# Two more blocks of the first mixer product, and one more down pair in each of the last two blocks, computed with seven products in place of eight, in an order given as a list

## The chip, the cores and the metric

The kernel runs on one core of a Trainium2 chip. The metric is the device time of one execution in microseconds (us), the median of three runs. Beside the runs there is one profiled execution. Its engines are TensorE (PE, with its weight loads PEld), VectorE (DVE), ScalarE (ACT), GpSimd (POOL) and SyncE (SP, which issues most DMAs).

## The reference

The input x has 2048 tokens of 512 channels. Linear attention over 32 heads of 16 channels is multiplied by a gate; the gate comes from a mixer that shifts channel groups along the tokens, and from an MLP with 1376 hidden channels behind it.

```python
xn = _layernorm(x)
s = _A_ref(xn, A_wqkv, A_wo)                       # linear attention, phi(t) = t+1 or exp(t), + 1e-6
g = _silu(_B_ref(xn, B_w1, B_w2, B_w3, B_w4))
return x + s * g

def _B_ref(x, w1, w2, w3, w4):
    h = _gelu(_layernorm(x) @ w1)                  # first mixer product
    ...                                            # its four groups of 128 channels, shifted +1, -1, +2, -2 tokens
    x1 = x + hs                                    # hs = shifted h @ w2
    return x1 + _gelu(_layernorm(x1) @ w3) @ w4    # up, down
```

## The kernel before

The 2048 tokens are cut into four **blocks** of 512 (`BT`), each of four tiles of 128. Every fp32 value that goes into a product is split into a rounded high half and a low half (`rounded`: ACT copies the high half, DVE subtracts it for the low one), and each product of two values is three matmuls: high by high, low by high, high by low (`products`). A matmul streams 512 or 256 columns.

Where a product can be cut into two by two quarters, `seven` (and its kin) forms seven products of sums of quarters in place of eight of the quarters themselves: the left sums are `s1` to `s4`, the right ones `t1` to `t4`, and three PSUM banks `pa`, `pb`, `pe` collect them in halves of 256 columns. Before the change this is done for keys and queries of blocks 1 to 3 (`keys_queries`, banks `pak`, `pbk`, `pek`), for the second mixer product (`mix2`, banks `pam`, `pbm`, `pem`), for the attention output, for the up products, and for as many **down pairs** of a block as `SEVENS = 0, 2, 3, 3` says (`stream` and `chain`, banks `a` and `uc`); the other down pairs go plainly (`plain`, 512 columns).

The first mixer product is plain in every block. `mix1(b, g)` makes one group of 128 channels: twelve matmuls of 512 columns into the bank `h`, over the four channel chunks, with the tokens read one or two places to the side, which is the shift; four columns beside each block hold the neighbours' tokens (`split_halo`). DVE multiplies the bank by the row `abc` of each token's scale (`ht<-h,abc`; `join_a` fetches that row, spread over the partitions, from the row `arow` in DRAM), and ACT takes the Gelu. `make_u(b)` before that subtracts the token means (`um`, fetched from `mrow`) from the turned tokens `xt`, splits them, and forms the sums `us`, which keys and queries of that block use. Layernorm's statistics come from DVE's batch-norm instructions (`moments`). The weights w1 are split once, their halves stored to DRAM (`W1D`) and fetched again for blocks 2 and 3 (`w1_for`).

The whole program is recorded as a list of operations (`Plan`), and `Plan.emit` puts them in order: it plans times from modelled durations, gives each operation a due time, nudges some by the table `SOONER`, and chooses buffers as they come free. `ORD` sets the order in which the parts of the first half are recorded. TensorE runs attention's first products and the mixer of block 0 first, then blocks 1 to 3, then the MLP of the blocks one after the other.

Of the kernel before, what the change touches and what calls it, by code (L numbers as in the profile page):

```python
# [15 lines left out]
P = 128  # L16
# [72 lines left out]
class Plan:  # L89
# [121 lines left out]
    def move(self, eng, out, src, kind, mb, reads, writes, emit):  # L211
        op = self.add(eng, .42 if eng == "SP" else .6, 0, reads, writes, emit, mb=mb)
        op.rate, op.tail = self.RATE[kind], self.TAIL.get(kind, 0.0)
        return op
# [13 lines left out]
    def gather(self, out, src, share=1.0, kind="gather"):  # L228
# [3 lines left out]
    RATE = {"load": 2.93, "fetch": 3.3, "half": 4.27, "row": 4.23, "turn": 5.4, "store": 2.45,  # L232
            "gather": 5.73, "quarter": 6.42}

    def landing(self, op, s, dma):

        soft = op.eng == "POOL"
        dma = max(dma, s + (.33 if soft else 0)) + op.mb * op.rate
        late = min(1.11, .68 * max(0.0, dma - s))
        return dma, max(dma + (1.36 if soft else 1.25) + late, s + (3.77 if soft else 1.97 if op.loads else 1.68)) + op.tail  # L240

    GAP = {"PE": .16, "ACT": .035, "DVE": .035, "POOL": .15, "SP": .035}
    BEGIN = {"PE": 1.0, "ACT": 2.0, "DVE": .8, "POOL": .8, "SP": .75}
    DMA0 = 2.2
    TABLE, EXTRA = 1.41, .22
    TAIL = {"row": .95}
    PATIENCE = 2.5
    COLD, COLD_TILL = 1.84, 5.8
    SAFE = 2.0
# [3 lines left out]
    def nudged(self, table):  # L253

        for n, k in zip(table[::2], table[1::2]):
            self.ops[n].due -= .25 * k
        self.backward()

    def deadlines(self, first):
        t = first  # L260
        for op in self.ops:
            if op.eng == "PE":
                op.nom = t
                t += op.busy
        for op in self.ops:
            op.due = op.nom if op.eng == "PE" else INF
        self.backward()
        for op in self.ops:
            op.at = max([p.at + p.lat for p in op.pre], default=0.0)
            if op.eng == "PE":  # L270
                op.at = op.nom
            elif any(t.psum for t in op.tiles):
                op.due = min(op.due, op.at + self.PATIENCE)
            elif op.soon:
                op.due = min(op.due, max(op.at, op.soon.at) + op.patience)
            elif op.due == INF and not op.post:
                op.due = op.at + op.patience
        self.backward()

    def backward(self):  # L280
        for op in reversed(self.ops):
            if op.eng != "PE":
                for o in op.post:
                    op.due = min(op.due, o.due - self.GAP[o.eng] - (6.0 + op.mb * 4 if op.mb else op.lat))

    def meets(self, op, slots, users):

        e = {o.eng for o in op.pre}
        n = Counter()
        for t in op.tiles:  # L290
            if t.ap is None and t.tag in slots and n[t.tag] < len(slots[t.tag]):
                e |= users.get((t.tag, slots[t.tag][n[t.tag]][1]), set())
                n[t.tag] += 1
        return len(e - {"ACT"}) > 1

    def emit(self, first, lead, reserve, window, ahead, table=()):
        self.deadlines(first)
        self.nudged(table)
        ops = self.ops
        waiting = {op: len(op.pre) for op in ops}  # L300
        avail = {e: [] for e in ("PE", "ACT", "DVE", "POOL", "SP")}
        for op in ops:
            op.ready = 0.0
            if not waiting[op]:
                avail[op.eng].append(op)
        pe = [op for op in ops if op.eng == "PE"]
        head = 0
        free = dict(self.BEGIN)
        slots = {tag: [(0.0, i) for i in range(n)] for tag, n in self.counts.items()}
        port, dma = 0.0, self.DMA0  # L310
        lock = [(-1.0, -1.0)] * 8
        under = [0.0] * 8, [0.0] * 8
        table = 0
        users = {}
        done = set()
        slip = 0.0
        left = len(ops)
        while left:
            while head < len(pe) and pe[head] in done:
                head += 1  # L320
            front = pe[head] if head < len(pe) else None
            slip = max(0.0, free["PE"] - front.nom) if front else INF
            best = None
            for e, cands in avail.items():
                picks = []
                low = INF
                for op in cands:
                    s = max(free[e], op.ready)
                    if op.mb:
                        s = max(s, under[e == "POOL"][0] + self.GAP[e])  # L330
                    s = max(s, op.floor)
                    if op.two and s < port:
                        s = port
                    if e == "POOL" and not op.mb and not op.two:
# [23 lines left out]
                    if not ok:  # L358
                        continue
# [1443 lines left out]
```

## Time and profile before

| | us |
|---|---|
| median of 3 runs (501.72, 501.77, 502.53) | 501.77 |
| the profiled execution's span | 501.2 |
| TensorE busy in it | 494.3 (99%) |
| VectorE busy | 440.9 (88%) |
| ScalarE busy | 388.9 (78%) |
| DMA moved | 116.69 MB |

The span is the time from the first to the last instruction of one profiled execution, of which we have one; the runs' times hold 0.57 us more at the median. Busy is the time in which an engine had an instruction of its own in work. A busy engine is the bound only where the others don't hold it up, so the share has to be read by stretch.

### The profile page before, as it was taken

The page shows a single profiled execution, that of the slowest core. Times are in us where ns is not written, and L with a number is a line of the kernel's source. Part 1 is how long each engine was busy: PE and PEld are TensorE (multiplying, and loading weights), DVE is VectorE, ACT ScalarE, POOL GpSimd, SP SyncE. Part 2 cuts the span into 40 slices and gives each one's busy share as a digit, 9 for nine tenths or more (in the row PEclk, how much of TensorE's full clock was granted, in tenths as well). Part 3 has the DMA queues.
Part 4 walks back from the last instruction along what each step waited for, and adds up shares of the span by engine and source line. Part 5 has one row for each costly group of instructions (what it writes and reads, how often), then busy time and mean ns, then how long its engine had stood idle before and what let it go on. Part 6 is the DMA issues. An engine that isn't in the chain of part 4 may idle for free.

```text
span 501.2 us, 9464 instructions
## 1 busy us (share of the span) xinstructions
PE 494.3 (99%) x3102; PEld 442.2 (88%) x3102; DVE 440.9 (88%) x944; ACT 388.9 (78%) x859; POOL 84.9 (17%) x97
## 2 busy tenths in 40 slices
PE   8999999999999999999999999999999999999996
PEld 6777887898888888899999989999899998999986
DVE  5989999999699995999999998897799969998364
ACT  5999899867798884977777579957699878977551
POOL 1344433131221122020100002200020200201100
PEclk9999999999999999999999999999999999999999
DMA  7949985479994799979897599978699887898604
GB/s 245 365 110 239 319 261 144 106 149 269 322 260 134 191 336 233 262 198 286 266 319 243 193 312 260 269 235 245 190 252 305 225 192 239 278 314 266 154 8 120
DMA packets 86989, 116.69 MB, mean 233 GB/s; under 512 B 8864, under 2 KB 41148, under 8 KB 86940
## 3 DMA queue, kind: packets, MB, share of 16 engines
q1 hardware_dynamic: 77004, 98.00, 60.3%
q0 software_dynamic: 9936, 18.09, 20.9%
q8 instruction: 24, 0.39, 0.3%
q14 instruction: 25, 0.20, 0.2%
HBM read 73.70 MB, written 32.91 MB: 213 GB/s over the span
## 4 chain that ended last, share of the span: by engine, by line
PE 88%; DMA 8%; SPq 1%; ACT 1%; issue 0%; DVE 0%; POOL 0%; DVEq 0%
PE a L151 15%; PE pb L151 11%; PE h L151 9%; PE pbk L151 7%; PE g L151 7%; PE acc L151 6%; PE pe L151 6%; DMA w1t<-in_w 5%; PE pbm L151 5%; PE pbs L151 4%; PE uc L151 3%; PE pek L151 3%; PE pa L151 3%; PE pem L151 2%; PE pes L151 2%; PE pak L151 2%
## 5 line engine op out<-in xcount | busy, mean ns | idle before, releaser
L230 POOL DMA_DIRECT2D th<-in_x x14 | 12.3, 926 | 164.4 <-DMA w_t<-w4t 75.6
L230 POOL DMA_DIRECT2D o<-x x16 | 14.1, 895 | 65.1 <-DVE o L198 48.0
L178 ACT ACT_TABLE_LOAD x18 | 23.1, 1283 | 0.3
L652 POOL TENSOR_TENSOR rs<-w,nhalf 128x4 f32<-128x4 f32 (+2 forms) x10 | 16.7, 1675 | 38.1 <-DVE w L203 38.1
L173 ACT ACTIVATE gf<-gf 128x256 f32<-128x256 f32 (+1 forms) x48 | 22.0, 469 | 1.2 <-DVE gf L198 0.8
L230 POOL DMA_DIRECT2D zacc<-kr x16 | 16.4, 1022 | 36.5 <-DMA zacc<-kr 13.2
L230 POOL DMA_DIRECT2D e<-x1d x12 | 10.6, 1084 | 62.0 <-DVE e L198 44.1
L208 DVE SCALAR_TENSOR_TENSOR kr<-kt,kr 128x512 f32<-128x512 f32 x16 | 11.0, 686 | 4.4 <-ACT kt L173 4.4
L173 ACT ACT_TABLE_LOAD x11 | 14.1, 1283 | 1.0 <-PEq L1794 0.8
L173 ACT ACTIVATE ht<-ht 128x512 f32<-128x512 f32 x16 | 9.8, 623 | 6.5 <-DVE ht L198 6.5
L646 DVE BATCH_NORM_STATS2 st<-o 128x6 f32<-128x512 f32 x16 | 10.6, 681 | 4.7 <-DMA o<-x 4.7
L198 DVE TENSOR_TENSOR e<-a,e 128x512 f32<-128x512 f32 (+1 forms) x17 | 9.7, 587 | 5.1 <-PE a L151 5.1
L198 DVE TENSOR_TENSOR th<-th,so 128x512 f32<-128x512 f32 (+1 forms) x17 | 10.9, 648 | 3.3 <-ACT th L173 3.3
L173 ACT ACTIVATE x<-x,nm,rs 128x512 f32<-128x512 f32 x16 | 12.9, 805 | 0.0
L173 ACT ACTIVATE p<-pe 128x256 f32<-128x256 f32 x20 | 7.6, 382 | 6.7 <-PE pe L151 6.5
L173 ACT ACTIVATE p<-pb 128x256 f32<-128x256 f32 x20 | 7.6, 381 | 6.7 <-PE pb L151 6.5
L173 ACT ACTIVATE y<-o,nm,rs 128x512 f32<-128x512 f32 x16 | 11.8, 804 | 1.2 <-DVE nm L208 1.2
L173 ACT ACTIVATE th<-e 128x512 f32<-128x512 f32 (+1 forms) x12 | 7.1, 608 | 7.1 <-DVE e L198 7.1
L208 DVE SCALAR_TENSOR_TENSOR pq<-pq,qr 128x512 f32<-128x512 f32 x12 | 8.2, 686 | 3.9 <-ACT pq L173 3.8
L198 DVE TENSOR_TENSOR ht<-h,abc 128x512 f32<-128x512 f32 x16 | 10.8, 681 | 0.4 <-PE h L151 0.4
L198 DVE TENSOR_TENSOR gf<-pb,p 128x256 f32<-128x256 f32 x20 | 8.4, 418 | 3.1 <-PE pb L151 3.0
L208 DVE SCALAR_TENSOR_TENSOR qz<-pq,zb 128x512 f32<-128x512 f32 x16 | 10.7, 684 | 0.2
(1868 smaller groups left out, 2285.1 us busy)
## 6 DMA issues: line engine op xcount, KB each, us to landing
w_s<-in_w SPq DMA_DIRECT2D x34, 256.0 KB, 4.8
w_t<-w4t SPq DMA_DIRECT2D x26, 256.0 KB, 4.5
w_b<-w4d SPq DMA_DIRECT2D x24, 256.0 KB, 5.3
x<-in_x SPq DMA_DIRECT2D x16, 256.0 KB, 6.3
zacc<-kr POOLq DMA_DIRECT2D x16, 256.0 KB, 4.8
o<-x POOLq DMA_DIRECT2D x16, 256.0 KB, 4.7
x1d<-o SPq DMA_DIRECT2D x16, 256.0 KB, 3.8
xt<-in_xt SPq DMA_DIRECT2D x15, 256.0 KB, 6.2
```

The costliest lines, as they stand in the source:

```text
L151: lambda: nc.tensor.matmul(out.get(), lhs.get(), rhs.get(), start=start, stop=stop, skip_group_check=more))
L173: nc.scalar.activation(out.get(), src.get(), func, scale=get(scale), **kw)
L178: op.warm = lambda: nc.scalar.activation(self.scr[1].get(), self.scr[0].get(), func)
L198: self.vec(eng, out, [a, b], lambda: self.e(eng).tensor_tensor(out.get(), a.get(), b.get(), op=op), True)
L208: lambda: self.nc.vector.scalar_tensor_tensor(out.get(), a.get(), get(s), b.get(), op0=op0, op1=op1),
L230: lambda: self.nc.gpsimd.dma_start(out.get(), get(src), accum_op=ALU.add))
L646: pl.add("DVE", .62, .69, [xv], [st], lambda: nc.vector.bn_stats(st.get(), xv.get()))
L652: lambda: g.tensor_tensor(out.get(), src.get(), nh.get(), op=ALU.pow))
```

## The change

In blocks 2 and 3, `mix1_pair(b, p)` makes two groups of 128 channels at once by `seven`: the token quarters and sums that keys and queries already use stand on the left, and seven forms of w1 on the right (`b11`, `t1`, `b21`, `t2`, `b22`, `t3`, `t4`, for each of two pairs `p`). `forms_w1` makes the four sums on DVE and stores them to `W1D`; `mix1_pair` fetches all seven forms of 512 columns for each pair and block, 14 fetches a block for 8 before. In block 1, `mix1_whole` stays plain; block 0 keeps `mix1` with the multiplication by `abc`.

So that the scale no longer has to follow the product, `make_u` multiplies the centred tokens by `abc`, and keys and queries of these blocks use another factor (`rk` for `rs1`). The tokens are read unshifted; the shift is made later by an offset into `ht`, whose ends are copied between neighbouring blocks (`edges`), and so `forms(b)` waits for the mixer of block b+1, and `ORD` puts the second mixer products later. The statistics of blocks 2 and 3 go from DVE to ACT (`totals`: two passes with a running sum each). `SEVENS` becomes 0, 2, 4, 4, and the last block holds back two groups of down products, not three (`keep`). `Plan.emit` no longer plans: it follows `ORDER`, a list of all operations, and `HOMES`, a list of buffers.

```diff
-    SEVENS = 0, 2, 3, 3
+    SEVENS = 0, 2, 4, 4
...
+    def totals(xv, t, mv):
+        m = mv.cols(0, 1)
+        pl.act(t, xv, AF.Copy, scale=1.0 / D, total=m)
+        k = -float(D) if t is xv else -1.0
+        pl.act(t, xv, AF.Square, scale=k, bias=m, total=mv.cols(1, 2))
...
+        a = piece(f"abc{b}")
+        o = EDGE + b * BT
+        pl.fetch(a, arow[:, o:o + BT].via(lambda ap: ap.to_broadcast([P, BT])), "row")
         for c in range(NC):
-            pl.tt(XT[b, c], XT[b, c], m, ALU.subtract)
+            pl.tt(XT[b, c], XT[b, c], m, ALU.add)
+            pl.tt(XT[b, c], XT[b, c], a, ALU.mult)
...
+    def edges(b, n):
+        t, d = HT[b, n], -SHIFT[ORDER[n]]
...
+    def mix1_whole(b, g):
+        ps = bank(f"h{b}_{g}")
+        products(ps, [HELD[0].chunk(c, g * P, (g + 1) * P) + ut(b, c, 2, 2 + BT) for c in range(NC)])
+        t = HT[b, ORDER.index(g)] = pl.new("p", f"ht{b}_{g}", F32, PIECE)
+        pl.act(t[:, 2:2 + BT], ps, AF.Gelu_apprx_tanh)
+
+    def mix1_pair(b, p):
...
+        w = {y: pl.new("p", f"w1{y}_{p}{b}", F32R, PIECE)[:, :512] for y in W1F}
+        for k, y in enumerate(W1F):
+            o = (p * len(W1F) + k) * 512
+            pl.fetch(w[y].f32, W1D[:, o:o + 512])
+        def prod(x, y):
+            return [(w[y].cols(c * P, (c + 1) * P), w[y].cols((2 + c) * P, (3 + c) * P)) + U[b][x][c] for c in range(2)]
+        ps = seven(f"g{b}_{p}", z, prod)
+        pl.act(z[0], z[0], AF.Gelu_apprx_tanh)
+        pl.act(hs[1], hs[1], AF.Gelu_apprx_tanh)
+        pl.act(hs[0].cols(TH, BT), ps, AF.Gelu_apprx_tanh)
...
+        for k in range(4):
+            hl = rounds(f"w1t{k}")
+            rounded(*hl, t[k])
+            for q in range(2):
+                keep_w1(f"t{k + 1}", q, None, hl[q])
...
-            moments(f"st{i}", v, mv1[:, 2 * i:2 * i + 2])
+            totals(v, v, mv1[:, 2 * i:2 * i + 2])
...
-        keep = 3 if last else 2
+        keep = 2
...
-    pl.emit(first=6.0, lead={"p": 14.0, "w": 14.0}, reserve={"p": 20, "w": 1}, window=12.0,
-            ahead=6.0, table=SOONER)
...
+    pl.emit(ORDER, HOMES)
```

TensorE's row at the entry of block 2's first mixer product, before. `h2_0` is the bank of its first group, `u2_*` are the split tokens, `w1_*` the halves of w1; the banks `pbk9` and `pek9` are those of keys and queries of the same block.

```order
L151 MATMUL pek9_1807<-wq_3h_228,us2_3l_1617 128x512
L151 MATMUL h2_0_1878<-u2_0h_1445,w1_0h_1627 128x512
L151 MATMUL h2_0_1878<-u2_0l_1503,w1_0h_1627 128x512
L151 MATMUL h2_0_1878<-u2_0h_1445,w1_0l_1633 128x512
L151 MATMUL h2_0_1878<-u2_1h_1453,w1_1h_1638 128x512
L151 MATMUL h2_0_1878<-u2_1l_1527,w1_1h_1638 128x512
L151 MATMUL h2_0_1878<-u2_1h_1453,w1_1l_1644 128x512
```

A group's matmuls stood there one behind another, 512 columns each, and began with the first half of w1.

TensorE's row at the same place, after. `peg2_0`, `pbg2_0` and `pag2_0` are the three banks of the pair's seven products, `us2_*` the sums, `w1t1_02` a form of w1.

```order
L151 MATMUL pek9_1598<-wq_3l_340,us2_3h_1540 128x512
L151 MATMUL peg2_0_1684<-us2_0h_1415,w1t1_02_1638 128x256
L151 MATMUL pek9_1598<-wq_3h_321,us2_3l_1543 128x512
L151 MATMUL pbg2_0_1692<-u2_0h_1400,w1b11_02_1472 128x256
L151 MATMUL pbk9_1522<-kq3_0h_870,u2_2h_1417 128x512
L151 MATMUL pbk9_1522<-kq3_0l_894,u2_2h_1417 128x512
L151 MATMUL pbk9_1522<-kq3_0h_870,u2_2l_1454 128x512
L151 MATMUL pbk9_1522<-kq3_1h_803,u2_3h_1413 128x512
L151 MATMUL pbk9_1522<-kq3_1l_915,u2_3h_1413 128x512
L151 MATMUL pbg2_0_1692<-u2_0l_1402,w1b11_02_1472 128x256
L151 MATMUL pbg2_0_1692<-u2_0h_1400,w1b11_02_1472 128x256
L151 MATMUL pag2_0_1701<-u2_2h_1417,w1b21_02_1316 128x256
```

The twelve matmuls of 512 columns for a group have become matmuls of 256 columns, spread among those of keys and queries; the first of all needs the form `t1`.

VectorE's row where block 1's tokens are centred, before (`um1` the means, `us1_*` the sums, `w1_*l` low halves of w1):

```order
L198 TENSOR_TENSOR xt1_0_328<-xt1_0_328,um1_507 128x512
L198 TENSOR_TENSOR xt1_1_336<-xt1_1_336,um1_507 128x512
L198 TENSOR_TENSOR us1_2_611<-xt1_0_328 128x256
L198 TENSOR_TENSOR us1_2_611<-xt1_1_336 128x256
L198 TENSOR_TENSOR w1_0l_620<-w1_s0_215,w1_0h_609 128x512
L198 TENSOR_TENSOR w1_3l_629<-w1_s3_202,w1_3h_592 128x512
L198 TENSOR_TENSOR w1_1l_639<-w1_s1_278,w1_1h_625 128x512
L198 TENSOR_TENSOR us1_2l_646<-us1_2_611,us1_2h_634 128x512
```

The sums stood right behind the first two subtractions.

VectorE's row there, after (`abc1` is the row of scales, `kq1_0` a form of the key and query weights):

```order
L198 TENSOR_TENSOR xt1_1_309<-xt1_1_309,um1_501 128x512
L198 TENSOR_TENSOR kq1_0_592<-wq_s2_181,kq0_0_555 128x512
L198 TENSOR_TENSOR xt1_2_293<-xt1_2_293,um1_501 128x512
L198 TENSOR_TENSOR xt1_1_309<-xt1_1_309,abc1_526 128x512
L198 TENSOR_TENSOR xt1_0_299<-xt1_0_299,um1_501 128x512
L198 TENSOR_TENSOR xt1_2_293<-xt1_2_293,abc1_526 128x512
L198 TENSOR_TENSOR xt1_0_299<-xt1_0_299,abc1_526 128x512
L198 TENSOR_TENSOR w1_0l_630<-w1_s0_250,w1_0h_618 128x512
L198 TENSOR_TENSOR us1_0_632<-xt1_0_299,xt1_2_293 128x256
L198 TENSOR_TENSOR us1_2_634<-xt1_1_309 128x256
L198 TENSOR_TENSOR w1_1l_636<-w1_s1_303,w1_1h_622 128x512
```

Behind each subtraction now stands a multiplication by `abc1`, and the sums and the low half of w1 come behind these.

SyncE's row where block 2's halves of w1 are fetched from DRAM, before (`x1d0` is a store of the mixer's result):

```order
L222 DMA x1d0_1476<-o3_1456 128x512
L222 DMA x1d1_1623<-o4_1497 128x512
L226 DMA w1_0h_1627<-w1d_600 128x512
L226 DMA w1_0l_1633<-w1d_600 128x512
L226 DMA w1_1h_1638<-w1d_600 128x512
```

The fetches stood in one row, with no store of w1 near them.

SyncE's row before block 2's first form arrives, after (`w1t1l`, `w1t0h` and the like are the halves of the four sums on their way to `W1D`, `w1t1_02` and `w1t2_02` forms fetched from there):

```order
L221 DMA w1d_705<-w1t0h_1532 128x256
L221 DMA w1d_705<-w1t3h_1576 128x256
L225 DMA w1b21_12_1581<-w1d_705 128x512
L221 DMA w1d_705<-w1t1l_1552 128x256
L221 DMA w1d_705<-w1t0l_1538 128x256
L221 DMA w1d_705<-w1t1h_1550 128x256
L221 DMA w1d_705<-w1t3l_1578 128x256 x2
L221 DMA w1d_705<-w1t3h_1576 128x256
L225 DMA w1t1_02_1638<-w1d_705 128x512
L221 DMA w1d_705<-w1t0h_1532 128x256
L221 DMA x1d0_1479<-o2_1303 128x512
L225 DMA w1t2_02_1643<-w1d_705 128x512
```

The fetch of a form stands right behind the stores that fill it, and the stores of the four sums lie among the fetches.

## Rows read from the trace of the kernel before

**Rows 1.** The page, span and busy time of each engine.

```profile
span 501.2 us, 9464 instructions
...
PE 494.3 (99%) x3102; PEld 442.2 (88%) x3102; DVE 440.9 (88%) x944; ACT 388.9 (78%) x859; POOL 84.9 (17%) x97
```

**Rows 2.** Waits of PE: total us, times, longest.

```profile
PE warm L151 <- POOL ones L548: 1.7, 1, 1.7
PE w1m L151 <- ACT w1mh L173: 0.6, 1, 0.6
PE h L151 <- ACT w_1h L173: 0.2, 1, 0.2
```

**Rows 3.** Windows: stretch and its length, busy us (instructions) by engine, PEclk, DMA share.

```profile
core 0: us, PE busy (x) PEld busy (x) DVE busy (x) ACT busy (x) POOL busy (x), PEclk, DMA share, GB/s
0.00:60.00 60.00, 57.41 (x238) 44.73 (x239) 51.76 (x108) 51.14 (x126) 20.32 (x30) 1.00 0.89 252
60.00:200.00 140.00, 140.00 (x729) 118.64 (x729) 125.47 (x275) 111.23 (x233) 36.75 (x37) 1.00 0.80 221
200.00:300.00 100.00, 100.00 (x662) 91.03 (x662) 99.70 (x211) 77.36 (x171) 5.85 (x6) 1.00 0.85 259
300.00:501.20 201.20, 196.86 (x1477) 187.78 (x1476) 163.97 (x353) 149.16 (x331) 21.93 (x25) 1.00 0.79 223
...
120.00:140.00 20.00, 20.00 (x108) 17.03 (x107) 14.69 (x35) 14.87 (x28) 3.67 (x4) 1.00 1.01 315
...
300.00:320.00 20.00, 20.00 (x172) 20.00 (x172) 17.33 (x39) 18.84 (x43) 4.40 (x5) 1.00 1.03 292
```

**Rows 4.** Chain that ended last, in order of time: start, us, work.

```profile
193.88 11.17 PE h L151 x48
...
384.62 2.96 PE a L151 x25
...
456.77 2.12 PE uc L151 x18
```

**Rows 5.** Groups by line: form, count, busy us, mean ns, idle before.

```profile
L198 DVE TENSOR_TENSOR ht<-h,abc 128x512 f32<-128x512 f32 x16 | 10.8, 681 | 0.4 <-PE h L151 0.4
...
L198 DVE TENSOR_TENSOR gf<-pb,p 128x256 f32<-128x256 f32 x20 | 8.4, 418 | 3.1 <-PE pb L151 3.0
...
L198 DVE TENSOR_TENSOR xt<-xt,um 128x512 f32<-128x512 f32 x12 | 8.0, 684 | 0.0
...
L646 DVE BATCH_NORM_STATS2 st<-xs 128x6 f32<-128x512 f32 x8 | 5.0, 678 | 0.0
...
L173 ACT ACTIVATE sq<-x,sx 128x512 f32<-128x512 f32 x4 | 2.8, 711 | 0.0
```

**Rows 6.** Timeline of DVE and PE, block 1, near 55 us: start, us, instruction.

```profile
53.41 0.68 DVE L198 TENSOR_TENSOR us_0l<-us,us_0h 128x512 fp32r<-128x512 f32 x1
54.02 0.68 DVE L198 TENSOR_TENSOR kq_1l<-kq,kq_1h 128x512 fp32r<-128x512 f32 x1
...
56.57 0.39 PE L151 MATMUL pek<-kq_0h,us_0l 128*128 128x512 f32 x1
```

**Rows 7.** DMA issues: count, KB each, median us to landing.

```profile
abc<-arow SPq DMA_DIRECT2D x4, 258.0 KB, 7.9
...
um<-mrow SPq DMA_DIRECT2D x3, 256.0 KB, 4.6
...
w4t<-w_1l SPq DMA_DIRECT2D x3, 256.0 KB, 9.6
...
w_0l<-w1d SPq DMA_DIRECT2D x2, 256.0 KB, 6.5
```

**Rows 8.** First weight tile of block 2: its fetch and its first products.

```profile
L151 PE MATMUL h<-u_0h,w_0h x4: 388/396/401, 137.8 to 144.4; 128*128 128x512 f32 x4
...
116.00 0.78 SPq L226 DMA_DIRECT2D w_0h<-w1d  x1
```

**Rows 9.** Chain that ended last, from its last products on.

```profile
494.94 2.02 PE a4x L151 x17
...
496.98 0.39 ACT th L173
...
497.86 0.42 DVE th L198
```

More of the change, by code (lines that the diff above doesn't have):

```diff
@@ L230, in gather @@
                          lambda: self.nc.gpsimd.dma_start(out.get(), get(src), accum_op=ALU.add))
[L232 to L249, printed above, removed]
     early = 0.0
     patience = 18.0
[L253 to L294, printed above, removed]
@@ L380, in emit @@
+    def emit(self, order, homes):
+        homes = iter(homes)
+        users = {}
+        table = 0
+        for n in order:
+            op = self.ops[n]
+            engs = {o.eng for o in op.pre}
             for t in op.tiles:
@@ L660, in scale_x @@
         w = small(f"w{lo}", n).all
-        pl.ts(w, var(mv1, lo, lo + n), EPS, None, ALU.add)
+        if lo < 2 * QT:
+            pl.ts(w, var(mv1, lo, lo + n), EPS, None, ALU.add)
+        else:
+            pl.ts(w, var(mv1, lo, lo + n), 1.0 / D, EPS, ALU.mult, ALU.add)
         power(r, w, n)
@@ L833, in feature_k @@
             ps = t
-        pl.act(r, ps, AF.Relu, scale=col(rs1, i))
-        pl.act(t, ps, AF.Exp, scale=col(rs1, i))
+        k = col(rk if centred else rs1, i)
+        pl.act(r, ps, AF.Relu, scale=k)
+        pl.act(t, ps, AF.Exp, scale=k)
         hi, lo = rounds(f"k{i}")
@@ new lines, in linear_attn_gated_by_mixer, with keep_w1, forms_w1 @@
+    W1F = "b11", "t1", "b21", "t2", "b22", "t3", "t4"
+    W1D = memory("w1d", 2 * len(W1F) * 512)
+    def keep_w1(y, k, c, v):
+        for p in range(2):
+            o = (p * len(W1F) + W1F.index(y)) * 512 + k * TH + (c or 0) * P
+            src = v.cols(p * P, (p + 1) * P) if c is not None else v.cols(p * TH, (p + 1) * TH)
+            op = pl.store(W1D[:, o:o + src.n], src.f32)
+            op.patience = 30.0
+            pl.soon(op)
+    def forms_w1():
+        r = HELD[0].raw
+        t = [piece(f"w1f{k}") for k in range(4)]
+        for c in range(2):
+            b11, b12, b21, b22 = (r[2 * k + c].cols(h * TH, (h + 1) * TH) for k in range(2) for h in range(2))
+            o = [v.via(lambda ap, c=c: ap.rearrange("p (q c w) -> p q c w", q=2, c=2)[:, :, c]) for v in t]
+            i = [v.via(lambda ap: ap.rearrange("p (q w) -> p q w", q=2)) for v in (b11, b12, b21, b22)]
+            for v, q in zip(o, t):
+                v.spans, v.n = [(c * TH, (c + 1) * TH)], TH
+            pl.tt(o[0], i[1], i[0], ALU.subtract)
+            pl.tt(o[1], i[3], o[0], ALU.subtract)
+            pl.tt(o[2], i[3], i[1], ALU.subtract)
+            pl.tt(o[3], i[2], o[1], ALU.subtract)
+        for k in range(4):
[3 more added lines that the diff above has]
+                keep_w1(f"t{k + 1}", q, None, hl[q])
@@ L1038, in mixer @@
     def mixer(b):
-        join_a(b)
-        for gg in ORDER:
-            mix1(b, gg)
-        forms(b)
+        if b < FIRST1:
+            join_a(b)
+            for gg in ORDER:
+                mix1(b, gg)
+            forms(b)
+            return
+        for n, gg in enumerate(ORDER) if b < SEVEN1 else ():
+            mix1_whole(b, gg)
+            edges(b, n)
+        for p in range(2) if b >= SEVEN1 else ():
+            mix1_pair(b, p)
+        if b == NQ - 1:
+            forms(b)
     x1d = [memory(f"x1d{b}", 512, QT * P) for b in range(NQ)]
@@ L1660, in linear_attn_gated_by_mixer @@
             pl.act(MQ[gg // 2][d].cols(gg % 2 * TH, (gg % 2 + 1) * TH), ps.cols(d * TH, (d + 1) * TH), AF.Copy)
-    M = {f"b{h + 1}{d + 1}": halves(f"m_b{h + 1}{d + 1}", in2(MQ[h][d])) for h in range(2) for d in range(2)}
+    M = {f"b{h + 1}{d + 1}": halves(f"m_b{h + 1}{d + 1}", in2(MQ[h][d])) for h, d in ((0, 0), (1, 0), (1, 1))}
     turn_y(0)
```

221 lines of the change are left out of this document (71 added, 150 removed), and 406 rows, old and new, of tables (HOMES, ORD, ORDER, SOONER).

## The prediction, made before the result was known

> **What bounds the kernel now.** I read the busy times first: TensorE works 494.3 us of a span of 501.2, while VectorE has 88% and ScalarE 78% [rows 1]. The reader should see that only 6.9 us of the span are not TensorE's. Next come its waits [rows 2]: the whole program has three worth naming, 1.7 us ahead of the first matmul, 0.6 for the centred w1, and 0.2 for block 0's mixer. Then the stretches [rows 3]: from 60 to 300 us TensorE is busy in all of it, at a granted clock of 1.00. Before 60 us it idles 60.00 − 57.41 = 2.6, of which 1.7 is the wait ahead of the first matmul, so 0.9 us are left. After 300 it idles 201.20 − 196.86 = 4.3, and the last matmul ends at 494.94 + 2.02 = 496.96, so 501.2 − 496.96 = 4.2 of these are the tail, in which ScalarE and VectorE finish the last tile [rows 9]. So the time is TensorE's work, plus 1.7 at the start, 0.9 in the front and 4.2 at the end. A change of TensorE's work shows in full as long as nothing else becomes late.
>
> **What TensorE's work costs.** A row of 48 matmuls of 512 columns takes 11.17 us, 232.7 ns each; 18 of 256 columns take 2.12, 117.8 each, and 25 take 2.96, 118.4 each [rows 4]. Two halves cost 235.6, only 1.2% more than a whole. The granted clock is 1.00 in every stretch [rows 3], that is 2.4 GHz, and no stretch loses TensorE's work, so I leave the clock as it is.
>
> **TensorE's part of the change.** Of the first mixer product, blocks 2 and 3 had 4 × 12 = 48 matmuls of 512 columns each, 96 in all. They become two pairs of groups a block, each seven products of six matmuls (two channel chunks, three halves' products): 84 of 256 columns a block, 168 in all. The fourth down pairs of blocks 2 and 3 go from plain to seven: in the two instruction orders bank `a` loses 42 of 512 columns, `a` and `a4x` together gain 39 − 3 = 36 of 256 columns, and `uc` gains 36. So 96 + 42 = 138 matmuls of 512 columns leave, and 168 + 36 + 36 = 240 of 256 columns come. The sum is 138 × 0.2327 = 32.11 out, 240 × 0.1178 = 28.27 in: −3.84 us. By the other row (118.4) the 240 cost 28.42 and the gain is 3.7; at exactly half of 232.7 they cost 27.92 and the gain is 4.2. I take 117.8, the longer chain's shape nearest to the new ones, and 3.7 to 4.2 as bounds.
>
> Two halves are 2.9 ns longer than a whole here (2 × 117.8 − 232.7), which is the price of the smaller shape. The Trainium skill, "TensorE: Matmul & The Clock Gate", section "Back-to-back issue gap", gives an isolated gap of N/2.4 + 2.5 ns, which would be 215.8 and 109.2 ns and a gain of 29.8 − 26.2 = 3.6 us (an estimate from that page): close to my sum, though both rows here are longer than its gaps.
>
> **VectorE's part.** A 512-column operation of VectorE costs 0.61 us from start to start (53.41 to 54.02 [rows 6]), a half one at most its duration, 0.42 [rows 5]. In the front, block 1 gains four multiplications of `xt` by `abc`, 4 × 0.61 = 2.4 us, ahead of the low halves that attention's keys and queries wait for. Before, the low half of the first sum ended at 54.09 and was first used at 56.57 [rows 6]: 2.5 us of lead. So 2.4 goes into 2.5, just so, and I cost it at nothing; the cover is thin and a rival stands on it. From 60 to 200 us there leave the eight batch-norm statistics of blocks 2 and 3 and twelve products `ht<-h,abc` of 512 columns, and there come eight `xt` multiplications and four low halves of w1's sums: −8 × 0.61. Twelve half additions in `seven` and eight half operations for w1's sums come: +20 × 0.42. Together +3.5 us against 140 − 125.47 = 14.5 idle there [rows 3]. From 200 to 300 us VectorE has 0.3 us idle and hardly gains or loses an operation by the orders (half operations for attention's forms less one), so its fullness stays TensorE's near neighbour but no later than before. After 300 the fourth pairs add about 12 half and 8 whole operations, 12 × 0.42 + 8 × 0.61 = 9.9, against 201.20 − 163.97 = 37.2 idle. Zero for all.
>
> **ScalarE's part.** Eight tiles get two passes each, 16 × 0.71 = 11.4 (the row of block 0's squares, [rows 5]); `seven` brings twelve half copies, at most 12 × 0.71 = 8.5. That is 20 against 140 − 111.23 = 28.8 idle in 60 to 200 [rows 3], and 56 small copies of neighbour tokens leave, which I do not credit. Zero, and it is off the path.
>
> **Queues.** SyncE gets 54 more DMAs: stores of w1's forms, and 28 fetches for 16 before. One stretch of their time already has a DMA share of 1.01 [rows 3]. Before, the first half of w1 was fetched at 116.00 and first used at 137.8 [rows 8], a lead of 21.8 us; a fetch lands in 6.5, a store in 9.6 [rows 7]. Now the form `t1` is stored shortly ahead of its own fetch, on one queue, so the fetch's wait for the store also holds back what is queued behind it on SyncE: further forms and stores of x1. Store and fetch together are 16.1, under 21.8 if the store goes out as early as the first fetch did, so I take zero here, with 16.1 as the other end.
>
> **The tail.** The last products are the same, and so are the ScalarE copy and the two halves of VectorE after them [rows 9]: zero. Sum: 501.2 − 3.84 = 497.36 of span. The runs' median is 0.57 above the profiled span; with that, **497.9**.
>
> **The rivals.**
> A, the forecast: −3.84, covers hold: 497.9 (497.6 to 498.1 by the bounds).
> B, the new order also closes gaps: 0.9 us of TensorE's idle time in the front [rows 2, 3] can go, since the order changes from the first rows on: 497.9 − 0.9 = 497.0. With the upper gain of 4.2 and half of the 1.7 us ahead of the first matmul, 501.77 − 4.2 − 0.9 − 0.8 = 495.9, rounded to 496.0. For it: work of other stages can stand in it. Against it: w1 still is centred through DMA, and the waits come from loads.
> C, VectorE is late in the front: the row `abc` lands 7.9 us after its issue, `um` 4.6 [rows 7], so the multiplication can start 3.3 later; 2.4 + 3.3 − 2.5 of lead = +3.2: 501.1, and the gain is nearly gone. For it: the lead is thin and VectorE has 51.76 busy of the first 60 us. Against it: `abc` of block 1 can be made early, since its statistics and those of `um` are the same.
> D, slower: block 2's mixer waits for its first form. If the store-to-fetch chain is exposed by the length of one fetch, 6.5 us, the time is 497.9 + 6.5 = 504.4; with all of it, 514.0. It turns into a loss from 3.9 us of exposure, and is measured as one from 4.9. For it: the order puts the fetch right behind its stores. Against it: 21.8 us of lead before, and TensorE has keys and queries of the block to do in the meantime.
> E, smaller matmuls cost more than the rows say: if each of the 240 had to wait for a weight load of the mean length, 442.2 / 3102 = 142.6 ns [rows 1], they would take 34.2, the sum would be +2.1, and the time 503.9. Against it: from 300 to 320 us 172 matmuls pass in 20.00 us at full load time, 116 ns each [rows 3].
> The Trainium skill, same page and section, has a rule of this kind: sustained pairs of load and matmul at about 131 ns for 512 columns and 81 for 128; some 98 for 256, an estimate between the two, would make the change 240 × 0.098 − 138 × 0.131 = 5.4 us slower. The trace contradicts it: 232.7 and 117.8 ns here.
> That the work isn't removed is excluded: the orders count 3078 matmuls and transposes before and 3180 after, which is +240 − 138.
>
> **How the numbers follow.** A has 0.62: each term is counted, and TensorE's rows have been without idle time for 240 us. B has 0.17, C 0.12, D 0.07, E 0.02. A and B hold 0.79, which leaves more than 2 in 10 out, so the range reaches to C: 496.0 to 501.1. A measurement of this kernel tells about 0.2% from no change, 500.77 to 502.77. Faster: A and B, 0.79. Same: C, 0.12. Slower: D and E, 0.09.
>
> **What would show it.** TensorE busy near 490.5 with nothing named in its waits past the front: A. A busy time up to 494 would make the prices wrong (E). Idle time before 60 us falling from 2.6 to 1.7: B; rising to 5 or 6, released by VectorE's `us` or `kq` halves of block 1: C. A wait of TensorE for `w1t1` by a DMA, near 130 us: D. Should TensorE be idle elsewhere from 60 to 300 us, I have overlooked a cover, most likely VectorE's from 200 to 300, which has 0.3 us to spare.

## The result

| | median us (runs) | lowest to highest | ratio to the kernel before, 95% interval |
|---|---|---|---|
| before | 502.12 (20) | 501.66 to 504.21 | |
| after | 504.42 (20) | 502.15 to 506.43 | 1.0042 (1.0030 to 1.0053) |

The changed kernel is slower by 2.3 us, where 4 us less were forecast, and it scatters more: half of the runs of the kernel before lie between 501.66 and 502.10, while the changed one is spread over 4 us. The page of the profiled execution, whose own run took 505.28:

```profile
span 503.3 us, 9798 instructions
...
PE 494.0 (98%) x3204; PEld 446.7 (89%) x3204; DVE 456.5 (91%) x977; ACT 399.0 (79%) x876; POOL 82.4 (16%) x98
```

TensorE's busy time has hardly moved from the 494.3 of [rows 1], though its matmuls are as counted (102 more instructions, +240 − 138). The prediction had named a busy time of 494 as the sign of E, that the small matmuls cost more. But a busy time takes in short stands between matmuls whose ends are modelled, so it can't settle this. The stretches, as in [rows 3]:

```profile
core 0: us, PE busy (x) PEld busy (x) DVE busy (x) ACT busy (x) POOL busy (x), PEclk, DMA share, GB/s
0.00:60.00 60.00, 57.91 (x236) 45.17 (x237) 53.33 (x111) 52.22 (x110) 18.68 (x28) 1.00 0.88 248
60.00:200.00 140.00, 139.64 (x783) 120.50 (x782) 128.48 (x279) 122.33 (x264) 29.59 (x33) 1.00 0.92 253
200.00:300.00 100.00, 100.00 (x696) 92.98 (x695) 99.50 (x216) 76.13 (x174) 11.93 (x12) 1.00 0.85 254
300.00:503.30 203.30, 196.42 (x1496) 188.05 (x1494) 175.19 (x375) 148.32 (x332) 22.16 (x25) 1.00 0.85 238
```

And TensorE's waits (total us, times, longest). In [rows 2] they ended with the mixer of block 0; the longest now lie far behind it:

```profile
PE warm L151 <- POOL ones L379: 1.2, 1, 1.2
PE a L151 <- ACT f_3a L173: 1.0, 1, 1.0
PE uc L151 <- DMA w_t<-w4t: 0.7, 1, 0.7
PE pb L151 <- ACT p L173: 0.6, 1, 0.6
PE k L151 <- ACT wk_0h L173: 0.5, 1, 0.5
PE pbg L151 <- DMA w1t<-w1d: 0.4, 1, 0.4
```

To part work from waiting I took, for each matmul of 512 or 256 columns, the time from its start to the next one's start, less the usual 231.8 ns (512 columns) or 116.9 (256 columns), and summed what is over 40 ns as **gaps**, in us. A matmul at a lower clock adds to the gaps too; in these three traces that is so in the first 11 us only:

| trace | 0 to 60 | 60 to 300 | 300 to 440 | after 440 | first to last start | less all gaps |
|---|---|---|---|---|---|---|
| before | 3.70 | 1.01 | 0.41 | 0.35 | 495.00 | 489.53 |
| after | 4.49 | 1.85 | 4.90 | 0.30 | 497.40 | 485.86 |
| after, second trace (`again`) | 3.41 | 1.68 | 4.17 | 0.14 | 495.07 | 485.67 |

So TensorE's work fell by 3.7 and 3.9 us, as priced, and 6.1 and 3.9 us of gaps came, of which 4.5 and 3.8 lie from 300 to 440 us. In the profiled pair: −0.4 for an earlier first matmul, −3.7 of work, +6.1 of gaps, +0.2 in the tail, +2.1 in all (501.2 to 503.3).

The other engines in the two stretches that matter, first before, then after (columns as above):

```profile
160.00:300.00 140.00, 140.00 (x864) 124.75 (x863) 131.44 (x278) 106.92 (x226) 15.07 (x18) 1.00 0.86 257
300.00:440.00 140.00, 139.92 (x1044) 133.27 (x1044) 126.07 (x274) 116.04 (x253) 15.83 (x18) 1.00 0.87 246
```

```profile
160.00:300.00 140.00, 140.00 (x924) 127.95 (x923) 138.57 (x303) 111.15 (x247) 18.29 (x20) 1.00 0.89 261
300.00:440.00 140.00, 137.52 (x1029) 130.70 (x1028) 122.52 (x260) 103.62 (x235) 15.27 (x18) 1.00 0.92 261
```

From 160 to 300 us VectorE's idle time fell from 8.6 us to 1.4. From 300 to 440, where the gaps are, VectorE and ScalarE are less busy than before; only the DMA engines are busier. So no compute engine is fuller there than it was.

### The profile page after: what moved, and what is told of

It reads as the page before. It is cut to its first block, busy times and chain, and to the rows that moved or that the text cites. A ratio compares the mean times of both kernels' runs of the same rounds, so it can differ in the third digit from the quotient of the medians.

```text
span 503.3 us, 9798 instructions
## 1 busy us (share of the span) xinstructions
PE 494.0 (98%) x3204; PEld 446.7 (89%) x3204; DVE 456.5 (91%) x977; ACT 399.0 (79%) x876; POOL 82.4 (16%) x98
## 4 chain that ended last, share of the span: by engine, by line
PE 77%; DVE 8%; DMA 7%; ACT 4%; issue 2%; SPq 1%; ACTq 0%; DVEq 0%
PE a L151 11%; PE g L151 8%; PE pb L151 8%; PE acc L151 5%; PE h L151 4%; PE pbk L151 4%; PE pbm L151 4%; PE pe L151 4%; PE uc L151 4%; PE pbs L151 4%; PE pek L151 2%; PE pbg L151 2%; PE pem L151 2%; PE pa L151 2%; PE k L151 2%
## 5 line engine op out<-in xcount | busy, mean ns | idle before, releaser
L491 POOL TENSOR_TENSOR rs<-w,nhalf 128x4 f32<-128x4 f32 (+2 forms) x10 | 14.2, 1420 | 30.1 <-DVE w L203 30.1
L173 ACT ACTIVATE u<-pb 128x256 f32<-128x256 f32 x20 | 7.6, 380 | 4.7 <-PE pb L151 4.7
L1365 DVE TENSOR_REDUCE den<-qz 128x32 f32<-128x512 f32 x16 | 10.8, 674 | 0.2
L208 DVE SCALAR_TENSOR_TENSOR pq<-pq,rd 128x512 f32<-128x512 f32 x16 | 10.7, 676 | 0.1
L198 DVE TENSOR_TENSOR gf<-pa,p 128x256 f32<-128x256 f32 x20 | 8.4, 419 | 2.4 <-PE pa L151 2.1
L198 DVE TENSOR_TENSOR gf<-u,pe 128x256 f32<-128x256 f32 x20 | 8.3, 415 | 2.3 <-PE pe L151 2.1
L173 ACT ACTIVATE pq<-qv,rk 128x512 f32<-128x512 f32 x12 | 8.3, 714 | 2.4 <-DMA q8d<-q8z 1.5
```

The costliest lines, as they stand in the source:

```text
L173: nc.scalar.activation(out.get(), src.get(), func, scale=get(scale), **kw)
L198: self.vec(eng, out, [a, b], lambda: self.e(eng).tensor_tensor(out.get(), a.get(), b.get(), op=op), True)
L208: lambda: self.nc.vector.scalar_tensor_tensor(out.get(), a.get(), get(s), b.get(), op0=op0, op1=op1),
L491: lambda: g.tensor_tensor(out.get(), src.get(), nh.get(), op=ALU.pow))
L1365: pl.add("DVE", .6, .68, [t], [den], lambda: nc.vector.tensor_reduce(den.get(), t.get().rearrange("p (h d) -> p h d", d=DH), axis=AX.X, op ...
```

## The experiments

Each run is compared with the kernel before on the same chip; its median there was 501.93 to 502.24. Names in the diffs are those of the changed kernel.

**Again, and the start.** The changed kernel as it is:

> The changed kernel once more, for a second trace of the same program beside the other runs of this call. TensorE lost some 6.3 us more between its matmuls than in the kernel before, of which 4.9 lie from 300 to 420 us and 2.3 ahead of 20 us. If those stalls are waits that the fixed order makes certain, the second trace has them at the same matmuls (the fetch of w_t near 312, f_3a near 396) and about the same sum. If they are chance meetings on the queues, they stand elsewhere and the sum moves by a microsecond or more with the time, which went from 502.15 to 506.43 in 20 runs. About 504.4 either way.

Measured: 503.67, ratio 1.0035 (1.0017 to 1.0052), profiled in a run of 502.92. The gaps from 300 to 440 stand at the same matmuls (1.06 near 311, 0.95 near 364, 1.86 near 395): their sum belongs to the program. (The places are less firm: in `warm3` below, with the same lists, the sum is 4.8, but next to nothing is lost at `f_3a` near 396, and 1.7 near 408.) Of the 2.3 us between the two traces, 1.1 lie ahead of 60 us, and they come from the start. First the changed kernel's first profile, then this one (start, us, instruction; `wk_s,xt` are products of unsplit values):

```profile
5.52 1.22 PE L151 MATMUL k<-wk_0h,u_0h 128*128 128x512 f32 x2 [0.50 <-ACT wk_0h L173]
6.54 0.63 PE L151 MATMUL k<-wk_0l,u_0h 128*128 128x512 f32 x1
6.96 1.91 PE L151 MATMUL k<-wk_s,xt 128*128 128x512 f32 x2
...
10.79 0.40 PE L151 MATMUL k<-wk_1h,u_1h 128*128 128x512 f32 x1
```

```profile
5.53 0.72 PE L151 MATMUL k<-wk_0h,u_0h 128*128 128x512 f32 x2 [0.86 <-ACT wk_0h L173]
...
6.59 1.02 PE L151 MATMUL k<-wk_s,xt 128*128 128x512 f32 x2
...
8.99 0.62 PE L151 MATMUL k<-wk_1h,u_1h 128*128 128x512 f32 x2
```

The same ten products need 5.3 us in the one and 3.5 in the other: 1.8 us between two executions of one program. From start to start a matmul of 512 columns takes 0.42 us in the first (6.54 to 6.96) and 0.23 later, so the first ran at the lower of TensorE's two levels (1.2 GHz) until about 9.9 us. The view prints a granted clock of 1.00 there in both, but the trace's record of that clock begins only 9.8 us into the span in the first and 4.2 us in the second, so the 1.00 ahead of it is no reading. Ahead of the products lie the warm matmuls and a pause of 0.50 us in the first trace and 0.86 in the second; the faster start has the longer pause, so its length doesn't decide. More matmuls ahead of it were tried:

```diff
+    once = pl.ops[-1].emit                            # the last warm matmul
+    pl.ops[-1].emit = lambda: [once() for _ in range(3)]
```

> The last of the matmuls ahead of the first weights is issued three times, some 0.9 us more of work, so that TensorE has no pause of 0.7 us before its first product. Theory 'slow start': after that pause the first products go at half speed until about 9.9 us, where in the kernel before they go at full speed from about 7; without the pause the program gains 1.2 to 2 us: 502.4 to 503.2, and the gaps ahead of 20 us fall from 7.1 to about 5. Rival: the start waits for its loads and the speed of the first products does not matter: 504.4 to 504.6.

Measured: 503.05, ratio 1.0021 (1.0010 to 1.0032), 502.38 to 504.66. The ten products took 3.5 us in its trace, as in `again`, though 0.4 us of the pause were left. Over all traces of the changed lists, the ten took 4.7 to 5.7 us in six of the nine without this edit and 3.5 in three; in the four with it (`fix1`, `fix2` and `fix3` below have it too) they took 3.5 to 3.7. So the edit steadies the start. The median is 0.6 us below that of `again` on the same chip and the scatter is 2.3 us in place of 4; the two intervals overlap, so the 0.6 is likely and not shown. The kernel before with the same edit:

> The kernel before with the same addition at the start as the run with three warm matmuls more. There the first products went at half speed until 7.0 us in the one trace that there is, in the changed kernel until 9.9 in one trace and not at all after 4.3 in another. If the change made the start worse, the kernel before gains at most 0.5 us by it: 501.7 to 502.2. If its start is as uncertain, it gains as much as the changed kernel did (0.6): 501.5.

Measured: 501.77, ratio 0.9996 (0.9987 to 1.0006): no difference that can be told. The start is at most a small part of what the change lost.

**VectorE ahead of 240 us.** The multiplications that the change added, cut down:

```diff
-            pl.tt(XT[b, c], XT[b, c], a, ALU.mult)
+            pl.tt(XT[b, c].cols(0, 8), XT[b, c].cols(0, 8), a.cols(0, 8), ALU.mult)
```

> The twelve multiplications of the centred tokens by their scales work on 8 of 512 columns; the rest is left out, so the tokens are not scaled. Order and buffers are as in the changed kernel. That takes 12 x 0.55 = 6.6 us from VectorE, 2.2 in the front and 4.4 from 100 to 200 us. Theory 'late VectorE': work added there pushes it into the stretch from 160 to 300 us, where it is full, and its lateness becomes gaps of TensorE from 300 to 420: those 4.9 us go for the most part, 500 to 501. Rival 'order': the list's leads are too short for what transfers and tables take, whatever VectorE has to do: at most 1 us goes, 503.4 to 504.4.

Measured: 504.32, ratio 1.0049 (1.0029 to 1.0068). Nothing is gained. Then the statistics of the mixer's result, cut down (`bn_less`) or doubled (`bn_more`):

```diff
-        moments(f"st2{i}", xv, mv2[:, 2 * i:2 * i + 2])
+        moments(f"st2{i}", xv.cols(0, 8), mv2[:, 2 * i:2 * i + 2])        # bn_less
...
+        twice = pl.ops[-2].emit                                           # bn_more
+        pl.ops[-2].emit = lambda: [twice() for _ in range(2)]
```

> The sixteen statistics of the mixer's result on VectorE read 8 of 512 columns; the rest is left out, so the second layernorm's statistics are of 8 channels. Order and buffers as in the changed kernel. In its trace VectorE has but one pause over 0.15 us from 172 to 315 us (in the kernel before, from 198 to 309). Thirteen of the sixteen lie after 118 us, so some 13 x 0.6 = 7.8 us leave ahead of and inside this stretch. Theory 'late VectorE': VectorE is behind at 300 us and its lateness is what stalls TensorE from 300 to 420; the gaps there fall from 4.9 to about 1, and the time to about 500.5. Rival 'short leads': the gaps stand at the places where the list puts an operation that waits for a transfer ahead of one that TensorE needs; they stay within 1 us of 4.9, and the time within 1 us of 504.

> The same sixteen statistics are each issued twice, 16 x 0.6 = 9.8 us more work of VectorE, of which some 7.8 after 118 us; nothing else changes. Theory 'late VectorE': most of it shows in the time, 508 to 512. Rival 'short leads': under 2 us show, 504 to 506.

Measured: `bn_less` 504.59, ratio 1.0041 (1.0028 to 1.0055), gaps from 300 to 440 of 5.2 us, at the same places and one more near 383; `bn_more` 512.94, ratio 1.0216 (1.0200 to 1.0231). VectorE has no room left ahead of 300 us, since nearly all of the added work shows (8.9 us of some 9.8), and its new gaps are there (10.4 us from 60 to 300). But taking work away ahead of 243 us does not shorten the gaps behind 300: from 243.8 to 311.2 us VectorE went on without a pause over 0.15 us in `bn_less` too. The runs speak against the half of 'late VectorE' that puts the blame ahead of 240 us, and leave the rest of it open. `dve_less` took out 5.7 of the 15.6 us that the change itself added to VectorE (busy 450.8 us for 456.5), so this part of the added work is not what costs.

**The order by the planner.** The lists replaced by the planner of before, without its nudges, for the changed work (`plan44`, shown), for the work before (`b_plain`), and for the work before with `SEVENS = 0, 2, 4, 4` and `keep = 2` (`b_plain44`). In the last two the kernel before loses its table `SOONER`:

```diff
-    pl.emit(ORDER, HOMES)
+    pl.emit(first=6.0, lead={"p": 14.0, "w": 14.0}, reserve={"p": 20, "w": 1}, window=12.0, ahead=6.0)
```

> The changed kernel's computation, put in order by the planner of the kernel before (due times and buffers from its model, without its table of nudges) in place of the two lists. Theory 'order': the work fits, only the list stalls; TensorE's gaps from 60 us on fall back to those of the kernel before, and the time is 498 to 500. Theory 'late VectorE': the work itself overfills VectorE, and any order stalls by several us: 503 to 508.

> The kernel before, put in order by its planner without the table of nudges: the control for the run in which the planner orders the changed kernel's work (545.9). If the planner alone is good for the work of before, 502 to 506, then the 545.9 say that the changed work is hard to order; if it needs its nudges, 520 and more, that run tells nothing of the work.

> The control with one part of the change alone: a fourth down pair of blocks 2 and 3 in seven products, and two groups of down products held back in the last block. By the matmuls, 42 of 512 columns leave and 72 of 256 come: 72 x 0.1178 - 42 x 0.2327 = -1.3 us against the control, if nothing gets late. If the added VectorE work and transfers of these pairs (some 10 us and 1.6 MB) make the MLP late, it is 0 to 4 us slower than the control.

Measured: 545.86, 537.53 and 544.48 (ratios 1.0863, 1.0710 and 1.0835). Without its nudges the planner loses 35 us on the old work as well, so these runs can't tell whether the changed work has a better order than the lists. They do bear out the prices once more: less all gaps, TensorE's work is 489.5 us in `b_plain`, 488.0 in `b_plain44` and 485.9 in `plan44`, so the fourth down pairs take off 1.5 (1.3 forecast) and the whole change 3.6. And `b_plain44`, which is one part of the change alone, is 7 us slower than its control, where −1.3 to +4 were expected: its gaps from 300 to 440 are 26.5 us for 17.6, and 24.5 in `plan44`. In an order that suits none of them, in which the granted clock was also 0.50 for 14 to 27 us in all, that points at the down pairs and shows no more.

**The places.** What a gap behind 300 us is made of, from the chain that ended last in the changed kernel's first profile (start, us, work):

```profile
387.96 0.62 DVE q8z L160
...
388.60 5.93 DMA q8d<-q8z
...
394.62 0.10 ACT pq L173
...
395.36 1.28 ACT L178
...
396.86 0.32 ACT f_3a L173
...
397.22 0.38 PE a L151
```

ScalarE's next exponentials (`pq11`) were given the buffer from which tile 8's turned queries (`q8z`) were still on their way to DRAM; they stood until that store had landed, then ScalarE changed its table, and only then made `f_3a`, for which TensorE waited. Nothing in this chain needs `q8z` but the buffer. Near 312 it is a form of w4, stored and fetched again. First the kernel before, then the changed one, SyncE and TensorE (start, us, instruction):

```profile
288.77 0.99 SPq L222 DMA_DIRECT2D w4t<-w_1l  x2
...
295.18 1.15 SPq L226 DMA_DIRECT2D w_t<-w4t  x2
...
314.23 0.51 PE L151 MATMUL uc<-w_t,f_0th 128*128 128x256 f32 x3
```

```profile
300.08 1.24 SPq L221 DMA_DIRECT2D w4t<-w_1l  x2
...
306.80 0.86 SPq L225 DMA_DIRECT2D w_t<-w4t  x2
...
312.88 0.71 PE L151 MATMUL uc<-w_t,f_0th 128*128 128x256 f32 x4 [0.69 <-DMA w_t<-w4t]
```

The first of these fetches stood 19 us ahead of the first product that uses such a form before, and stands 6.1 us ahead now, just about its landing time. The stores that fill the form had landed by about 304 us. What the fetch waited for is in the chain that ended last of the changed kernel:

```profile
300.74 0.60 DVE th L198
302.07 4.67 DMA out<-th
306.80 5.94 DMA w_t<-w4t
312.88 0.83 PE uc L151 x5
```

The list gives the form the buffer of a gated tile `th`, and SyncE stood 4.0 us until the store of that tile had landed. So here too a buffer was given out while a store from it was still under way. One buffer exchanged (`swap`), and small moves (`fix1`, then `fix2` with two of the moves changed; both have the addition at the start in them):

```diff
+SWAPS = (('pq11', 19), ('w1t2_02', 16))               # swap: the first alone
+MOVES = (([3390, 3393, 3391, 3394, 3395, 3392, 3397, 3398], 3447), ([4162, 3885], 3905),
+         ([4693, 4696, 4702, 4697, 4703], 4492))      # fix2: operations, and the one that they go behind
```

> The changed kernel with one entry of the buffer list exchanged: the exponentials of tile 11's queries (pq11) go to another buffer than the one that the turned queries of tile 8 (q8z) still hold until their store has landed; nothing else changes. In the changed kernel ScalarE stands 1.5 us at that place with f_3a behind it, and TensorE waits 1.2 us near 396. Theory 'short leads': the wait at 396 goes, but the next things that are due there (the halves q8s0h, near 409) come by a chain of their own through DRAM and are as late as before, so part of the 1.2 us comes back there: 503.2 to 504. Rival 'buffers': the reuse of buffers alone holds TensorE up, and the whole goes: 502.5 to 503.

> The changed kernel with the same operations and small moves in its two lists at the places where TensorE stood in every trace: three warm matmuls more at the start; another buffer for pq11 and for the fetch of w1t2; five products that need the fetched form t2 near 312 put behind eleven others; ScalarE's copy p12 near 364 put ahead of qr8 and th6; nine products of the next up pair near 408 put ahead of those that need q8s0h. Theory 'short leads': of some 6.5 us of gaps after 60 us, 3 to 4 go, and 0.5 at the start: 499.8 to 501.2, faster than the kernel before (502.2). Rival: something else is full (VectorE from 172 to 315, or the queues), the gaps come back at the next place, and it stays within 1 us of 504.

> As fix1, but with other moves at the two places where fix1 still stood or stood longer: near 312 eight products that need fetched forms go behind thirteen others, and near 408 five products of the down pairs, which need no bank of their own, go ahead of those that need q8s0h, in place of the next up pair, whose bank was still held and which cost fix1 3.2 us. Theory 'short leads': gaps after 60 us fall from some 6.5 to 3 or 4, and the time to 501 to 502. Rival 'something is full': the gaps stay above 5.5 in sum wherever they stand, and the time is 503.5 or more.

Measured: `swap` 504.63, ratio 1.0047 (1.0029 to 1.0064), no gap at `f_3a`, but 0.9 behind 400 and 2.1 near 312, and no gain in time; `fix1` 505.15, ratio 1.0069 (1.0049 to 1.0089), with 3.2 us lost near 407, where products had been pulled ahead into a bank that was still held (its trace is of its slowest run, 507.98, and behind that stand the granted clock was 0.50 from 410.7 to 414.1); `fix2` 503.37, ratio 1.0024 (1.0012 to 1.0036), gaps from 300 to 440 of 3.9, which is no better than `warm3` with the addition at the start alone. A gap that is closed comes back in part at the next place, so there is not one wrong entry in the lists.

**VectorE and the transfers behind 240 us.** In place, with the same lists: gates and queries on VectorE cut down (`dve_mlp`), GpSimd's adding transfers cut down (`dma_mlp`), and both.

```diff
-        pl.tt(t, a, t, ALU.add)                                     # dve_mlp, and five like it
+        pl.tt(t.cols(0, 8), a.cols(0, 8), t.cols(0, 8), ALU.add)
...
-        pl.gather(th, x[i * P:(i + 1) * P, :])                      # dma_mlp, and two like it
+        pl.gather(th.cols(0, 8), x[i * P:(i + 1) * P, :8])
```

> The changed kernel's lists, with VectorE relieved behind 240 us: the additions and multiplications of the gates of blocks 0 to 2 and two of the operations on each tile's queries work on 8 or 16 of 512 columns, the rest is left out. Some 24 gate operations and 28 of the queries at 0.5 us each, 26 us of VectorE. Theory 'full VectorE': the gaps of TensorE from 300 to 440 us (4.2 to 4.9 in three traces of these lists) come from VectorE's queue; they fall under 1.5, and the time to 500 to 501. Rival 'short leads': each gap is a transfer's or a table's own length behind the operation before it; they stay over 3, and the time over 502.5.

> The changed kernel's lists, with GpSimd's adding transfers of the last stage (x into the gated tiles, the mixer's result into the down products) on 8 of 512 columns; the rest is left out. Some 26 transfers of 256 KB leave, which took 8 us each where one held a buffer that TensorE's chain needed. Theory 'short leads, held by transfers': the gaps from 300 to 440 fall by 1.5 us or more, since buffers and queues come free earlier: 502 to 503. Theory 'full VectorE': no change, 503.7 to 504.5.

> Both edits of the last two runs at once: VectorE relieved of some 26 us and GpSimd's adding transfers cut to 8 columns, both behind 240 us; the rest of that work is left out. Alone they gave 501.64 and 502.73, where the changed kernel takes some 504. If the gaps are chains that run through VectorE's queue and a transfer in turn, the two gains add up: 2.4 and 1.3, to 500 to 500.8, with gaps from 300 to 440 under 1.5. If both close the same gaps, it stays at 501.3 to 501.8.

Measured: `dve_mlp` 501.64, ratio 0.9988 (0.9972 to 1.0005); `dma_mlp` 502.73, ratio 1.0007 (0.9994 to 1.0021); both 500.59, ratio 0.9971 (0.9959 to 0.9984), four of nine runs between 499.85 and 499.99. Against the 504.04 between the two medians of the changed kernel, 504.42 and 503.67, that is 2.4, 1.3 and 3.5 us: the gains add up. Some 0.2 us of each lie outside the span: a run is 1.9 us longer than its span in the changed kernel, and 1.7 in these three and in the kernel before. In the spans' medians the gains are 2.2, 1.1 and 3.2. `dve_mlp` met neither of its two ranges, and the intervals of `dma_mlp` and `again` just overlap (1.0021 and 1.0017). Of TensorE's waits in the changed kernel one is left behind 300 us in `both_mlp`:

```profile
PE a L151 <- ACT f_3a L173: 0.9, 1, 0.9
```

Its gaps from 300 to 440 are 2.7 us, as many as in `dma_mlp`, and under 1.5 was expected. But its trace is of its slowest run (502.66, with a slow start: 5.4 us for the ten products), and that of `dve_mlp` too (504.10, gaps of 4.0), so for these two the times, not the traces, carry the verdict. The kernel before has 0.4 there, so it should have little to gain by such relief; that was not run. What was cut here is also work that both kernels have, not what the change added: the runs show that the gaps hang on VectorE and on transfers, and not that the added work made them.

**With the whole computation.** `fix2`, with the multiplication of the gated tiles of blocks 0 to 2 moved to GpSimd:

```diff
-        pl.tt(th, th, so, ALU.mult)
+        pl.tt(th, th, so, ALU.mult, eng="POOL")
```

> fix2 with its whole computation, and the twelve multiplications of the gated tiles of blocks 0 to 2 on GpSimd in place of VectorE: 12 x 0.6 = 7 us leave VectorE behind 285 us, about a quarter of what dve_mlp left out. Theory 'chains through VectorE and transfers': a quarter of its 2.3 us, 0.6: 502.6 to 503.0, gaps from 300 to 440 some 3. Rival: GpSimd's longer multiplication and its queue, which also issues the adding transfers, delay the tiles' buffers more than VectorE gains: 503.4 to 505.

Measured: 510.44, ratio 1.0166 (1.0152 to 1.0180). GpSimd's and VectorE's rows at the same moment (start, us, instruction):

```profile
300.61 1.95 POOL L202 TENSOR_TENSOR th<-th,so 128x512 f32<-128x512 f32 x1
```

```profile
299.36 1.28 DVE L202 TENSOR_TENSOR w_1l<-w_fb,w_1h 128x512 fp32r<-128x512 f32 x2
300.56 2.56 DVE L202 TENSOR_TENSOR w_0l<-w_fa,w_0h 128x512 fp32r<-128x512 f32 x1
303.05 0.41 DVE L202 TENSOR_TENSOR gf<-u,pe 128x256 f32<-128x256 f32 x1
```

The low half `w_0l` takes 0.68 us elsewhere and 2.56 here: it ends 0.6 us behind GpSimd's multiplication, not beside it. VectorE's busy time rose from 455.7 us in `fix2` to 457.6, though twelve instructions left. So the relief was none, and the longer chains cost 7 us, all of it gaps of TensorE. No run that keeps the whole computation of the changed kernel is faster than the kernel before.

## Why the prediction was wrong

- **TensorE's price was right.** −3.84 was forecast, −3.7 and −3.9 is what the two traces show between the gaps. The bound by weight loads (E) did not come, though its sign, a busy time near 494, did.
- **VectorE's amount was right, its cover was not.** The terms +2.4, +3.5 and +9.9 make 15.8; its busy time rose from 440.9 to 456.5, by 15.6. The step that failed is "Zero for all": idle time was summed over long stretches and set against the added work, and nothing was to be late behind it. In its place 3.8 to 4.5 us of gaps came from 300 to 440. 11.5 us from 60 to 200 and 28 behind 300 were still idle afterwards, and TensorE waited all the same, since what counts is by how much each operand is early at its place. From 172.4 to 311.9 us VectorE had one pause over 0.15 us (before: none from 198.5 to 309), and what it makes near the end of that stretch came 11 us later than before: the forms of w4 go to DRAM at 300.08 in place of 288.77. The added work ahead of 240 us is not to blame by itself, as `dve_less` and `bn_less` say.
- **The queues were taken at zero by a lead read from the kernel before.** A fetch 21.8 us ahead [rows 8] was measured under the planner; nothing said that the lists keep such leads. They don't: 6.1 us ahead in place of 19 for the form of w4, 3.3 in place of 21.8 for the form `t1` itself (fetched at 122.08, used at 125.4), and buffers given out while a store was still under way, at 312 and at 396. This is the second zero that failed. The prediction saw the fetch right behind its stores in the order, and still took the kind end of the term.
- **Rival D had part of the mechanism and the wrong place.** Block 2's first forms cost 0.4 us (`pbg` behind `w1t`); the fetch of w4's form near 312 cost 1.0, and two more chains, through ScalarE's queue near 364 and a buffer near 396, cost 1 to 2 each. It was priced as one exposure of 6.5 to a form's own store, and it is several of about 1, two of them behind the store of another tile in the buffer. That D's time of 504.4 is the measured median is luck: its number came from another place. The sum of the gaps, +4 us or more, is what turned the sign.
- **Rivals B and C** were about the front. TensorE's gaps there went from 3.7 to 4.5 and 3.4 in two traces. Most of that lies in the first 11 us (2.0 before, 3.3 and 1.6 after), where the level of the clock at the start decides; the rest (1.7 before, 1.2 and 1.9 after) hardly moved, so neither a filled gap nor a late `abc` shows.
- **The 0.57 us outside the span** set one execution's span against other executions' times. Where both are of one run, it is 1.7 in the kernel before (500.3 and 502.03) and 1.9 to 2.0 in the changed one. The forecast was made against the median, so only 0.2 us of it came in.

What is shown: the work fell as priced; the gaps behind 300 us are the program's own, two of their chains run through a buffer that waits for a store, and both less work on VectorE and fewer transfers behind 240 us shorten the time, each by its own part. What is not shown: why the lists are that tight. A fuller VectorE and more transfers may have left no better order, or the lists may simply not be the best ones for this work; no other good order of it was run. The lists hold for one set of operations only, so neither part of the change could be undone alone under them.

## What to carry to other kernels

When an engine is busy 99% of the time, work taken from it pays only as far as everything that feeds it can come earlier by as much. So read, chain by chain, how long the operands near the change lie ready before their use, and do not set added work against the idle time of a stretch. A fetch through DRAM, or a buffer that waits for a store, needs its lead at each place (4.7 to 5.9 us in the chains above). Where an order is given as a list, look for buffers that are handed out while a store from them is under way. Count gaps from the start of one matmul to the next; a busy share hides them.

## What the runs showed of the hardware

A VectorE subtraction of 512 columns took 2.56 us in place of 0.68 while GpSimd multiplied two operands, and ended 0.6 us after it. In that trace (`fix3`) the five VectorE operations with both inputs in SBUF that began beside such a multiplication took 1.17 to 2.94 us in place of 0.41 or 0.68, while those that read a PSUM bank kept their 0.41 to 0.69. The Trainium skill, "GPSIMD Engine Reference", section "1. Specifications", says that GpSimd shares its SBUF interfaces with VectorE and that the two contend where VectorE has two inputs from SBUF; the rows agree. And one program's first ten products took 5.3 us in one execution and 3.5 in another, by the level of TensorE's clock. The rows print a granted clock of 1.00 for both, because the record of that clock begins later, at 9.8 and 4.2 us.
